# GateLoop attention and a squared-ReLU FFN on one core: scores as 64 by 64 tiles, the last store on SyncE, a new order for the first part

## The chip, the core and the metric

The kernel runs on one core of a Trainium2 chip. A core has a matrix engine (TensorE, "PE" in the profile, with its weight loads as "PEld"), VectorE (DVE), ScalarE (ACT), GpSimd (POOL) and SyncE (SP), which only issues transfers and waits. Each works through its own list of instructions in order and waits for others by semaphores. The metric is the device time of one execution in microseconds, the median of the runs.

## The reference

The first part is a linear attention with a complex gate for each step and channel; its result, rearranged, is the input of a two-layer FFN.

```
q, k, v, a_re, a_im: (B, H, S, D) = (4, 8, 768, 48), fp32
scale = min(|a|, 0.999) / (|a| + 1e-6);  a = (a_re + i a_im) * scale
for t in range(S):
    S_state = a[t] * S_state + k[t] outer v[t]      # complex state, (D, D) per head
    y[t]    = q[t] @ real(S_state)
x = y as (B*S, H*D) = (3072, 384)
h = relu(x @ w_in)            # w_in: 384 x 2048
out = (h * h) @ w_out         # w_out: 2048 x 384
```

The two weights come in double precision and are turned into fp32 on the core ("decoding"): each element is two 32-bit words.

## The kernel before

A sequence is cut into 6 chunks of 128 steps. Two sequences go together as a "group": there are 12 groups (`gi`), each with two chunks (`b` = 0 and 1), so 24 chunks. The first group of each pair of sequences begins with an empty state. The channels lie on the partitions as two heads of 48 rows, each in a half of 64 rows (`rows(hh)`); with four pairs of heads (`p_` = 0 to 3) all eight heads are there. The last pair lies in the gaps of the other three and is copied out of them into `last` by a transfer (`last_heads`, L901).

For each chunk the function `chunk` makes:

- `scores` (a0, b0): unless the chunk is the first of its sequence, the states' products `y` (L936), 16 matmuls of 48 rows by 64 columns; then the scores `a_ps` (L944), 16 matmuls of 48 rows by 128 columns, two parts of a complex product for four pairs and two heads.
- `keys_turned` and `keys_copied` (a1 to a4): transposes of the keys into `tp` (L951) and ScalarE's copies into `kt`.
- `masked` (a5): VectorE multiplies the scores by the causal mask.
- `sums_of_values` (a6), `tokens` (a7, ScalarE's copies into `x`), `added` and `new_state` (a8, a9).

Each fp32 matmul instruction leaves two records in the trace, so the 16 scores of a chunk are 32 records.

`make_operands` makes queries and keys with the gates' running products: 31 steps (tokens `o` for a whole group, `p` and `q` for the first and second half of the first two groups). Its last products, p30 and q30, release the transposes, the scores and the heads' copy (p21, q21).

The FFN follows group by group: `g` fills the gaps of `x` by a transfer (L1039), `F` is the first product `h_ps` (L1047 for the first two groups, L1063 later), `H` the squared ReLU (L1070, L1071), `T` or `Z` the second product (L1083, L1153), `R` its evacuation (L1026, L1029), `s` the store (L1117). X, Y and Q are sums on VectorE that save a part of the second product. In the first part of the run the weights are decoded block by block: `f` and `j` load the words (L692, L688), U and S are ScalarE's two steps (L618, L625), D and A VectorE's two (L632 and an addition at L494). `w` and `W` read the weights again to check their range; `K` reduces the check to one number, `count`.

The order of everything is one string, `FRONT`, that is followed token by token; each token adds its instructions to the lists of the engines that it uses, and the lists are kept in that order. `l` and `i` load the group's operands into `raw`, `v` loads the values into `vt`, and M0 to M8 are preparations: M0 is one small activation that brings in ScalarE's table for the reciprocal root, M1 makes the mask by two ScalarE copies with a transpose between, M2 to M8 are VectorE's memsets.

At the end each engine loads `count`, compares and branches past a general path (L1362, L1363) that these inputs do not take. Behind the branch SyncE goes through the semaphores of all queues and engines. The last group's second output tile is stored in two halves, of which ScalarE's queue issues the one that is ready last.

Of the kernel before, what the change touches and what calls it, by code (L numbers as in the profile page):

```python
# [32 lines left out]
ROWS = 64  # L33
LEVELS = 7
HALF = 64
RE, IM = 0, 1
# [390 lines left out]
def quotient_path(ctx, tc, feat, vtok, w_in, w_out, w1, w2, out, n_seq, count):  # L427

    nc = tc.nc
    N, _, D, _, NP, C = feat.shape  # L430
    DM, FF = w_in.shape
# [31 lines left out]
    def rows(hh):  # L463
        return head_rows(hh, D)
# [450 lines left out]
    def chunk(gi, b):  # L915
# [7 lines left out]
        def scores():  # L923
            qk = qk_of[gi % 2]

            def operand(i, p_, at):
                return last[gi % 2][at, b, i, 0:C] if p_ == NG else qk[at, b, p_, i, 0:C]

            ys = tiles["y"] = [py.tile([P, NP, C], F32, tag="y", name="y") for _ in range(2)]
            ps = tiles["ps"] = pa.tile([C, HH, NP, C], F32, tag="a", name="a_ps")  # L930
            if not first:
                for two in range(0, NP, 2):
                    for c in (RE, IM):
                        for hh in range(HH):
                            for p_ in (two, two + 1):
                                nc.tensor.matmul(  # L936
                                    ys[p_ % 2][crossed(hh, p_), p_ // 2],
                                    lhsT=states[b][1 - c_seq % 2][rows(hh), c, columns(hh, p_ * ROWS + PAD)],
                                    rhs=operand(c, p_, rows(hh)),
                                    start=(p_ < 2 and c == RE), stop=False, skip_group_check=True)  # L940
            for p_ in range(NP):
                for c in (RE, IM):
                    for hh in range(HH):
                        nc.tensor.matmul(ps[:, hh, p_], lhsT=operand(2 + c, p_, rows(hh)),  # L944
                                         rhs=operand(c, p_, rows(hh)), start=(c == RE),
                                         stop=(c == IM))

        def keys_turned(c):
            tp = tiles["tp"] = pm.tile([C, NG, P], F32, tag="m", name="tp")
# [161 lines left out]
    def store(i, b):  # L1111

        queue, cols = nc.sync, slice(0, DM)
        if i == NGR - 1 and b:
            queue, cols = (nc.scalar, slice(0, MH)) if b == 1 else (nc.sync, slice(MH, DM))
        b = min(b, 1)
        queue.dma_start(out=in_turn(out, groups[i][b])[:, :, cols], in_=out_of[i, b][:, cols])  # L1117

# [38 lines left out]
    def outputs(i, r):  # L1157
# [27 lines left out]


    FRONT = (
        "M8 l0.0.0 M2 M3 M7 l0.0.1 M1 M0 p0.0 p0.1 p0.3 p0.4 p0.5 p0.7 p0.2 q0.0 q0.3 p0.8 p0.9 "
        "p0.10 q0.4 q0.5 p0.11 q0.7 l0.1.0 f0 f1 l0.1.1 v0.0 f2 i0.1.0 j0 j2 q0.1 p0.12 p0.22 "
        "q0.8 q0.2 U0 q0.9 p0.6 q0.10 S0 p0.15 p0.23 p0.24 D0 p0.25 M4 p0.13 M5 p0.16 q0.11 "  # L1190
        "p0.26 i0.1.1 j1 D1 p0.27 A0 p0.17 p0.14 j3 i1.2.0 U1 S1 U2 q0.12 p0.18 q0.6 S2 q0.22 "
        "A1 f4 l1.2.0 f3 j4 p0.19 q0.15 p0.20 q0.23 p0.28 q0.24 p0.29 q0.25 p0.30 q0.16 D2 "
        "q0.26 q0.13 q0.27 A2 q0.17 p0.21 f6 a0.1 a0.2 U3 q0.14 a0.0 a0.3 U4 S3 q0.18 p1.6 a0.4 "
        "S4 a0.5 a0.6 l1.2.1 a0.7 D3 q0.19 M6 a0.8 q0.28 q0.20 p1.0 p1.3 q0.29 D4 q0.30 i1.2.1 "
        "q1.0 p1.4 p1.5 j6 j5 p1.1 p1.2 j7 g0.0 f5 v0.1 q0.21 f7 p1.7 p1.10 p1.9 p1.8 A3 A4 "
        "F0.1.0 U5 a0.9 U6 S5 D5 b0.1 b0.0 p1.11 b0.2 p1.12 S6 H0.1.0 A5 U7 b0.3 b0.4 S7 p1.15 "
        "D6 p1.23 b0.5 F0.0.0 b0.6 b0.7 f8 p1.24 A6 p1.25 q1.3 p1.16 D7 p1.26 A7 p1.27 D8 p1.17 "
        "F0.2.0 H0.0.0 q1.4 H0.2.0 U8 p1.22 S8 F0.3.0 b0.8 H0.3.0 p1.18 p1.13 p1.14 A8 g0.1 f11 "
        "F0.2.1 f9 f10 v1 p1.19 p1.20 p1.28 D9 p1.29 p1.30 q1.5 U9 q1.1 H0.2.1 q1.7 D11 b0.9 "
        "D10 F0.3.1 T0.0.0 H0.3.1 S9 A9 U10 q1.8 S10 q1.9 q1.2 q1.10 F0.0.1 F0.1.1 p1.21 f12 "  # L1200
        "f13 A10 q1.6 U11 q1.11 q1.12 S11 U12 a1.0 a1.1 T0.1.0 a1.5 a1.6 a1.7 S12 D13 D12 A11 "
        "q1.15 q1.23 A12 T0.2.0 T0.3.0 a1.2 U13 H0.0.1 q1.22 H0.1.1 a1.3 T0.4.0 q1.24 q1.25 "
        "q1.16 q1.26 q1.13 q1.27 q1.17 f14 g1.0 f15 S13 q1.14 l2 F1.2.0 H1.2.0 A13 F1.0.0 "
        "F1.3.0 q1.18 a1.4 U14 H1.3.0 U15 S14 i2 S15 q1.19 q1.28 q1.20 q1.29 D14 q1.30 A14 D15 "
        "A15 q1.21 a1.8 T0.5.0 F1.1.0 T0.6.0 T0.7.0 o2.0 o2.1 o2.3 o2.4 E0.0 o2.5 o2.2 b1.0 "
        "o2.7 a1.9 b1.5 T0.0.1 T0.1.1 b1.3 T0.2.1 b1.6 T0.3.1 T0.4.1 T0.5.1 T0.6.1 T0.7.1 o2.8 "
        "o2.9 o2.10 H1.1.0 b1.7 s0.0 v2 g1.1 w0 o2.11 o2.12 o2.15 o2.22 o2.13 o2.6 H1.0.0 "
        "F1.0.1 F1.1.1 E0.1 o2.14 b1.4 H1.1.1 l3 T1.0.0 b1.1 H1.0.1 F1.3.1 T1.1.0 T1.2.0 T1.3.0 "
        "T1.4.0 T1.5.0 T1.6.0 T1.7.0 o2.23 o2.24 o2.25 o2.16 o2.26 o2.27 o2.17 o2.18 o2.19 "
        "o2.28 o2.20 o2.29 o2.30 F1.2.1 o3.0 o3.6 o3.3 o3.4 o3.5 b1.2 o3.7 E1.0 b1.8 b1.9 o2.21 "  # L1210
        "a2.0 a2.5 t0 a2.1 T1.0.1 T1.1.1 o3.2 o3.1 o3.8 a2.2 o3.10 o3.9 a2.3 a2.6 a2.4 a2.7 "
        "H1.2.1 o3.11 o3.12 W0 a2.8 b2.0 a2.9 o3.22 H1.3.1 b2.5 T1.2.1 T1.3.1 b2.6 T1.4.1 "
        "T1.5.1 T1.6.1 b2.7 T1.7.1 g2 F2.0 o3.13 o3.15 o3.23 o3.24 o3.25 o3.16 o3.26 o3.27 "
        "o3.17 o3.14 H2.0 o3.18 o3.19 o3.28 o3.20 o3.29 o3.30 F2.2 H2.2 F2.4 H2.4 l4 s1.0 b2.1 "
        "F2.1 o4.0 H2.1 o3.21 s0.1 v3 F2.6 H2.6 b2.2 o4.3 F2.5 F2.7 o4.2 o4.4 o4.5 H2.7 X2.0 t1 "
        "X2.2 Y2.2 t3 H2.5 Y2.0 o4.7 b2.3 a3.0 b2.4 E1.1 s1.1 X2.1 Y2.1 a3.5 Z2.1 b2.8 a3.6 "
        "o4.1 o4.8 o4.9 Q2.0 b2.9 a3.3 a3.7 o4.10 a3.4 o4.11 F2.3 H2.3 Z2.0 a3.1 b3.0 X2.3 R2.0 "
        "o4.6 o4.22 Z2.3 a3.2 b3.5 b3.6 b3.7 o4.12 Y2.3 o4.13 Q2.3 Q2.1 o4.15 o4.23 Q2.2 o4.24 "
        "a3.8 a3.9 Z2.2 R2.3 Z2.5 o4.14 R2.2 R2.5 R2.1 o4.25 o4.16 o4.26 o4.27 o4.17 g3 F3.2 "
        "H3.2 F3.0 b3.3 b3.4 Z2.4 H3.0 o4.18 o4.19 o4.20 o4.28 o4.29 o4.30 F3.4 H3.4 F3.6 R2.4 "  # L1220
        "H3.6 X3.2 X3.0 F3.5 F3.1 b3.1 H3.5 F3.7 w1 l5 o5.0 t2 Z2.6 o5.3 o5.1 o5.4 H3.1 b3.2 "
        "o5.5 R2.6 o5.7 X3.1 o4.21 s2.1 s2.0 W1 w2 v4 F3.3 H3.3 H3.7 o5.2 Z3.0 b3.8 a4.0 X3.3 "
        "b3.9 Y3.1 Y3.2 a4.1 a4.5 Y3.0 Z3.1 R3.0 o5.6 o5.9 a4.2 o5.8 a4.3 Q3.0 o5.10 R3.1 o5.11 "
        "Q3.2 Y3.3 a4.6 a4.4 a4.7 a4.8 b4.0 a4.9 b4.1 Z3.2 Z3.3 o5.12 o5.22 b4.2 W2 b4.3 b4.4 "
        "R3.2 b4.5 b4.6 R3.3 b4.7 b4.8 o5.15 o5.23 o5.24 o5.25 Q3.1 Q3.3 o5.16 o5.13 Z3.4 Z3.5 "
        "w3 g4 o5.14 R3.4 o5.26 R3.5 F4.5 H4.5 l6 o5.27 o5.17 o5.18 o5.19 o5.20 v5 o5.28 F4.1 "
        "H4.1 X4.1 o5.29 F4.0 F4.4 o5.30 H4.0 o6.0 W3 H4.4 o6.3 b4.9 F4.3 Z3.6 H4.3 o6.4 F4.2 "
        "H4.2 o6.5 R3.6 o6.2 o6.1 F4.6 o6.7 H4.6 o5.21 s3.0 a5.0 F4.7 s3.1 o6.9 o6.8 a5.5 a5.6 "
        "o6.10 a5.7 H4.7 Z4.0 b5.0 Z4.1 Y4.1 o6.11 X4.3 Y4.3 X4.0 o6.6 w7 o6.22 o6.12 W7 R4.0 "
        "b5.5 X4.2 o6.15 Y4.0 Q4.0 R4.1 b5.6 Y4.2 Q4.1 Z4.2 R4.2 b5.7 o6.23 o6.24 Q4.2 o6.25 "  # L1230
        "o6.16 Z4.3 o6.13 Q4.3 o6.26 Z4.4 R4.3 Z4.5 R4.5 o6.27 o6.17 R4.4 o6.14 g5 F5.2 H5.2 "
        "o6.18 F5.4 F5.0 H5.4 o6.19 o6.28 o6.20 o6.29 o6.30 F5.3 Z4.6 l7 w6 H5.0 W6 a6.3 F5.1 "
        "o7.1 R4.6 H5.3 H5.1 F5.6 o7.0 H5.6 a6.4 X5.0 o7.3 o7.4 o7.5 F5.7 s4.0 o6.21 w8 v6 F5.5 "
        "a6.0 v7 a6.1 Z5.0 H5.5 W8 H5.7 o7.2 a6.2 w4 s4.1 X5.2 a6.5 Y5.0 Y5.2 o7.7 a6.6 a6.8 W4 "
        "o7.9 o7.8 R5.0 o7.10 b6.0 w9 W9 a6.7 Z5.1 X5.1 a6.9 b6.5 Q5.0 X5.3 Q5.2 Y5.1 Y5.3 R5.1 "
        "o7.11 Z5.2 o7.12 b6.3 R5.2 b6.4 Z5.3 b6.1 Z5.4 Q5.3 o7.15 o7.23 o7.24 o7.25 Q5.1 o7.16 "
        "w5 R5.3 b6.2 o7.22 W5 R5.4 b6.6 b6.8 Z5.5 Z5.6 b6.7 w10 g6 F6.1 o7.13 o7.26 o7.27 R5.5 "
        "o7.14 o7.6 o7.17 o7.18 o7.19 o7.28 o7.20 o7.29 o7.30 H6.1 F6.6 F6.5 l8 R5.6 H6.6 W10 "
        "v8 o7.21 s5.0 w14 s5.1 H6.5 F6.2 H6.2 F6.0 o8.0 o8.2 H6.0 b6.9 X6.2 Y6.2 o8.3 F6.4 "
        "a7.1 F6.3 o8.4 o8.5 H6.3 o8.6 H6.4 a7.0 a7.5 X6.1 a7.2 F6.7 H6.7 o8.1 X6.0 o8.7 o8.8 "  # L1240
        "o8.10 Z6.0 a7.3 R6.0 o8.9 Z6.1 Y6.0 X6.3 Y6.3 Y6.1 Q6.0 Q6.2 Z6.2 a7.4 W14 a7.6 a7.7 "
        "R6.2 a7.8 o8.11 a7.9 b7.0 Q6.3 R6.1 b7.5 w13 W13 o8.12 b7.1 b7.2 o8.22 Z6.3 R6.3 o8.13 "
        "o8.15 Q6.1 o8.23 o8.24 b7.6 b7.3 Z6.4 b7.7 b7.4 g7 o8.14 Z6.5 o8.25 R6.5 o8.16 o8.26 "
        "o8.27 o8.17 R6.4 b7.8 F7.5 F7.0 H7.5 o8.18 H7.0 F7.1 w15 W15 H7.1 l9 F7.4 o8.19 o8.28 "
        "o8.20 o9.0 H7.4 F7.2 F7.6 H7.2 o8.29 X7.1 o8.30 o9.3 o9.4 o9.5 o9.7 Y7.1 o9.1 Z6.6 "
# [150 lines left out]
```

## Time and profile before

| | |
|---|---|
| Median of 3 runs | 664.95 us (664.7 to 665.57) |
| The profiled execution | 666.06 us |
| Its span, first to last instruction | 664.1 us |
| Granted TensorE clock, mean | 0.996 |
| Busy, PE / DVE / ACT / POOL | 616.7 / 493.2 / 434.9 / 31.9 us |
| First transpose of keys | 35.55 us |
| Last matmul begins its group | 655.34 us |

The page divides the span into 40 slices of 16.6 us and gives the busy tenths of each engine. A row of the timeline has the start, the length, the engine, the line, the operation with its output and inputs, how many instructions it merges, and in brackets how long the engine had been idle before it and what ended that. Matmuls overlap, so the length of a merged row is not the sum of its parts; the distance of starts is what counts. Transfers have their own rows at the time of their issue (SPq, ACTq, POOL).

### The profile page before, as it was taken

The numbers are of one execution on the slowest core, as the hardware profiler recorded it, in microseconds if no ns is written. First come the engines' busy times: TensorE is split into PE (matmuls) and PEld (weight loads), VectorE is DVE, ScalarE is ACT, GpSimd is POOL, SyncE is SP. The second block draws the span as 40 slices with busy tenths as digits, with TensorE's granted clock in tenths as the row PEclk, the third lists the DMA queues.
The fourth block names the chain that finished last, engine by engine and source line by source line (L and its number), as shares of the span: only waits on it lengthen the run. The fifth ranks groups of instructions, "written<-read, shape, count | busy, mean of one in ns | idle before, by whom it ended". The sixth has DMA issues, their size and how long they took to land.

```text
span 664.1 us, 13108 instructions
## 1 busy us (share of the span) xinstructions
PE 616.7 (93%) x5147; PEld 552.0 (83%) x5147; DVE 493.2 (74%) x981; ACT 434.9 (65%) x847; POOL 31.9 (5%) x74
## 2 busy tenths in 40 slices
PE   0068999999999999999999999999999999999996
PEld 0057987776889899989899899899999899989996
DVE  4999888979997969858849948968849858753030
ACT  7668989757584585494586785686685675644331
POOL 5230110000000000000000000000000000000000
PEclk9998999999999999999999999999999999999999
DMA  8986863540634331730842813542631620232101
GB/s 198 167 160 148 257 192 68 92 56 21 95 72 82 55 87 32 119 73 10 142 142 55 142 51 79 96 109 72 113 95 32 108 65 21 67 84 79 47 26 30
DMA packets 41744, 60.41 MB, mean 91 GB/s; under 512 B 5832, under 2 KB 29896, under 8 KB 41672
## 3 DMA queue, kind: packets, MB, share of 16 engines
q1 hardware_dynamic: 39360, 55.39, 38.7%
q0 software_dynamic: 1824, 3.64, 3.0%
q8 instruction: 42, 0.69, 0.5%
q10 hardware_dynamic: 488, 0.44, 0.2%
q14 instruction: 30, 0.25, 0.1%
HBM read 48.76 MB, written 4.72 MB: 81 GB/s over the span
## 4 chain that ended last, share of the span: by engine, by line
PE 91%; DVE 5%; DMA 2%; ACT 1%; issue 1%; ACTq 0%; POOL 0%; DVEq 0%; SPq 0%
PE h_ps L1063 31%; PE o_ps L1153 28%; PE a_ps L944 7%; PE o_ps L1083 6%; PE h_ps L1047 6%; PE y L970 4%; PE y L936 3%; PE add L994 3%; PE tp L951 2%; DVE ab L494 1%; DMA last<-qk 1%; DVE pr L494 1%; DMA raw<-in_feat_dram 1%; DVE qk L494 0%; DMA words<-in_moe_w_in_dram 0%
## 5 line engine op out<-in xcount | busy, mean ns | idle before, releaser
L1063 PE MATMUL h_ps<-x,w 128*128 128x256 f32 x960 | 212.4, 379 | 0.0
L1063 PEld LDWEIGHTS h_ps<-x,w 128*128 128x128 f32 x960 | 180.9, 190 | 24.1 <-ACT h L1070 0.2
L1153 PE MATMUL o_ps<-w,h 128*128 128x192 f32 x640 | 110.5, 328 | 0.0
L1153 PEld LDWEIGHTS o_ps<-w,h 128*128 128x128 f32 x640 | 103.8, 190 | 1.9 <-issue 0.5
L1070 ACT ACTIVATE h<-h_ps 128x512 f32<-128x512 f32 x80 | 47.5, 594 | 69.5 <-PE h_ps L1063 67.3
L494 DVE TENSOR_TENSOR pr<-ab 128x384 f32<-128x384 f32 (+3 forms) x196 | 70.1, 375 | 4.3 <-ACT ab L833 0.9
L1153 PE MATMUL o_ps<-w_sum,mix 128*128 128x192 f32 x320 | 55.3, 328 | 0.0
L494 DVE TENSOR_TENSOR a<-a_ps,mask 128x1024 f32<-128x1024 f32 x24 | 29.3, 1222 | 33.6 <-PE a_ps L944 33.5
L494 DVE TENSOR_TENSOR ab<-pr 128x48 f32<-128x48 f32 (+3 forms) x210 | 49.9, 260 | 5.3
L1153 PEld LDWEIGHTS o_ps<-w_sum,mix 128*128 128x128 f32 x320 | 51.7, 190 | 0.7 <-issue 0.2
L1071 ACT ACTIVATE h<-h 128x512 f32<-128x512 f32 x80 | 50.5, 631 | 2.5
L951 PE MATMUL tp<-ident,qk 128*128 128x128 f32 x120 | 21.5, 291 | 30.3 <-DVE qk L494 30.0
L1047 PEld LDWEIGHTS h_ps<-x,w 128*128 128x128 f32 x384 | 45.6, 197 | 4.0 <-DVE w L494 1.3
L1047 PE MATMUL h_ps<-x,w 128*128 128x128 f32 x384 | 46.4, 281 | 2.2 <-DMA x<-x 1.1
L494 DVE TENSOR_TENSOR qk<-ab,qk 128x768 f32<-128x768 f32 (+1 forms) x56 | 46.1, 842 | 1.0
L1083 PE MATMUL o_ps<-w,h 128*128 128x384 f32 x128 | 44.3, 492 | 0.0
L951 PEld LDWEIGHTS tp<-ident,qk 128*128 128x128 f32 x120 | 14.8, 146 | 35.3 <-issue 31.7
L981 ACT COPY x<-y 64x256 f32<-64x256 f32 (+1 forms) x72 | 26.5, 368 | 24.9 <-PE y L970 23.4
L944 PE MATMUL a_ps<-qk 48*128 48x128 f32 x576 | 39.9, 287 | 0.0
L494 DVE TENSOR_TENSOR mix<-h 128x256 f32<-128x256 f32 x40 | 16.8, 420 | 30.9 <-ACT h L1071 30.9
L758 ACT ACTIVATE qk<-raw 128x768 f32<-128x768 f32 (+1 forms) x28 | 37.4, 1341 | 3.6 <-DVE raw L494 3.6
L494 DVE TENSOR_TENSOR room<-ab,carry 128x1344 f32<-128x1344 f32 (+1 forms) x28 | 36.8, 1354 | 3.6 <-ACT carry L874 2.8
(106 smaller groups left out, 923.4 us busy)
## 6 DMA issues: line engine op xcount, KB each, us to landing
raw<-in_feat_dram SPq DMA_DIRECT2D x40, 288.0 KB
words<-in_moe_w_out_dram SPq DMA_DIRECT2D x8, 768.0 KB
again<-in_moe_w_in_dram SPq DMA_DIRECT2D x16, 384.0 KB
again<-in_moe_w_out_dram SPq DMA_DIRECT2D x16, 384.0 KB
last<-qk SPq DMA_DIRECT2D x48, 97.5 KB
words<-in_moe_w_in_dram SPq DMA_DIRECT2D x8, 576.0 KB
vt<-in_vtok_dram SPq DMA_DIRECT2D x24, 192.0 KB
out_dram<-o SPq DMA_DIRECT2D x23, 192.0 KB
```

Of the source, the lines that this page charges most:

```text
L494: nc.vector.tensor_tensor(out=out, in0=in0, in1=in1, op=op)
L758: nc.scalar.activation(out=out.rearrange("p c j n -> p c n j"), func=AF.Copy, in_=in_.rearrange("p c (n j) -> p c n j", j=L), **kwargs)
L944: nc.tensor.matmul(ps[:, hh, p_], lhsT=operand(2 + c, p_, rows(hh)), rhs=operand(c, p_, rows(hh)), start=(c == RE), stop=(c == IM))
L951: nc.tensor.transpose(tp[:, g], qk_of[gi % 2][:, b, g, 2 + c, 0:C], ident)
L970: nc.tensor.matmul(tiles["y"][p_ % 2][crossed(hh, p_), p_ // 2], lhsT=v[:, columns(hh, at)], rhs=tiles["am"][:, hh, p_], start=(first and ...
L981: nc.scalar.copy(out=x_of[gi][to, odd::2, b * C:(b + 1) * C], in_=tiles["y"][odd][of, 0:NP // 2])
L1047: nc.tensor.matmul(ps[:, j], lhsT=w1_blocks[:, k, g, at:at + P], rhs=x_of[i][:, g, b * C:(b + 1) * C], start=(g == 0), stop=(g == NG - 1))
L1063: nc.tensor.matmul(ps[:, j], lhsT=w1_blocks[:, k, g, at:at + P], rhs=x_of[i][:, g], start=(g == 0), stop=(g == NG - 1))
L1070: nc.scalar.activation(out=h, in_=h_ps[i, f], func=AF.Relu, scale=of_w1)
L1071: nc.scalar.activation(out=h, in_=h, func=AF.Square)
L1083: nc.tensor.matmul(o_of[i, b], lhsT=tokens_of(i, f, b)[:, j], rhs=w2[:, k], start=(k == 0), stop=(k == NFB - 1))
L1153: nc.tensor.matmul(to, lhsT=x(k)[:, j], rhs=factor(z)[:, 2 * k + j], start=(z in (0, 1, 3) and k == j == 0), stop=(k == KH // 2 - 1 and j ...
```

## The change

It has three parts in the code. The scores' product is split into two halves of 64 columns each, so that each of the 16 matmuls becomes two, one for each half of the output partitions. The half store that ScalarE issued is issued by SyncE. And the first part of `FRONT`, up to the end of group 3's work, stands in another order; from `g4` on it is the same. Its description also names a warming of ScalarE's table ahead of the mask's copies.

```diff
             for p_ in range(NP):
                 for c in (RE, IM):
                     for hh in range(HH):
-                        nc.tensor.matmul(ps[:, hh, p_], lhsT=operand(2 + c, p_, rows(hh)),
-                                         rhs=operand(c, p_, rows(hh)), start=(c == RE),
-                                         stop=(c == IM))
+                        for s in (slice(0, ROWS), slice(ROWS, C)):
+                            nc.tensor.matmul(ps[s, hh, p_],
+                                             lhsT=operand(2 + c, p_, rows(hh))[:, s],
+                                             rhs=operand(c, p_, rows(hh)), start=(c == RE),
+                                             stop=(c == IM), skip_group_check=True)
...
         queue, cols = nc.sync, slice(0, DM)
         if i == NGR - 1 and b:
-            queue, cols = (nc.scalar, slice(0, MH)) if b == 1 else (nc.sync, slice(MH, DM))
+            cols = slice(0, MH) if b == 1 else slice(MH, DM)
         b = min(b, 1)
...
     FRONT = (
-        "M8 l0.0.0 M2 M3 M7 l0.0.1 M1 M0 p0.0 p0.1 p0.3 p0.4 p0.5 p0.7 p0.2 q0.0 q0.3 p0.8 p0.9 "
-        "p0.10 q0.4 q0.5 p0.11 q0.7 l0.1.0 f0 f1 l0.1.1 v0.0 f2 i0.1.0 j0 j2 q0.1 p0.12 p0.22 "
-        "q0.8 q0.2 U0 q0.9 p0.6 q0.10 S0 p0.15 p0.23 p0.24 D0 p0.25 M4 p0.13 M5 p0.16 q0.11 "
-        "p0.26 i0.1.1 j1 D1 p0.27 A0 p0.17 p0.14 j3 i1.2.0 U1 S1 U2 q0.12 p0.18 q0.6 S2 q0.22 "
-        "A1 f4 l1.2.0 f3 j4 p0.19 q0.15 p0.20 q0.23 p0.28 q0.24 p0.29 q0.25 p0.30 q0.16 D2 "
-        "q0.26 q0.13 q0.27 A2 q0.17 p0.21 f6 a0.1 a0.2 U3 q0.14 a0.0 a0.3 U4 S3 q0.18 p1.6 a0.4 "
-        "S4 a0.5 a0.6 l1.2.1 a0.7 D3 q0.19 M6 a0.8 q0.28 q0.20 p1.0 p1.3 q0.29 D4 q0.30 i1.2.1 "
-        "q1.0 p1.4 p1.5 j6 j5 p1.1 p1.2 j7 g0.0 f5 v0.1 q0.21 f7 p1.7 p1.10 p1.9 p1.8 A3 A4 "
-        "F0.1.0 U5 a0.9 U6 S5 D5 b0.1 b0.0 p1.11 b0.2 p1.12 S6 H0.1.0 A5 U7 b0.3 b0.4 S7 p1.15 "
-        "D6 p1.23 b0.5 F0.0.0 b0.6 b0.7 f8 p1.24 A6 p1.25 q1.3 p1.16 D7 p1.26 A7 p1.27 D8 p1.17 "
+        "l0.0.0 l0.0.1 M1 M0 p0.0 p0.1 p0.3 p0.4 p0.5 p0.7 M2 M3 p0.2 q0.0 q0.3 M8 M6 M7 p0.9 "
+        "p0.8 q0.4 p0.10 q0.5 p0.11 l0.1.0 f0 f1 f2 i0.1.0 j0 j2 q0.1 p0.12 q0.7 p0.15 D0 p0.23 "
+        "p0.24 p0.25 U0 q0.10 p0.6 p0.22 q0.8 p0.13 S0 q0.9 q0.2 p0.14 p0.16 A0 U2 p0.26 M5 j1 "
+        "i0.1.1 U1 S1 S2 D2 p0.27 q0.11 p0.17 j3 i1.2.0 j4 q0.12 p0.18 D1 q0.15 p0.19 l0.1.1 "
+        "q0.22 f3 l1.2.0 v0.0 f5 q0.23 p0.28 q0.24 M4 p0.20 q0.25 p0.29 q0.16 p0.30 q0.26 q0.13 "
+        "q0.27 p0.21 f4 a0.1 a0.0 A1 q0.17 a0.5 A2 q0.14 q0.6 p1.6 a0.2 U3 a0.3 a0.4 q0.18 S3 "
+        "a0.6 l1.2.1 q0.19 U4 a0.7 S4 D3 D4 A3 i1.2.1 j5 j6 j7 a0.8 p1.0 q0.28 p1.3 q0.20 q1.0 "
+        "D5 q0.29 q1.3 q0.30 U5 p1.4 p1.5 g0.0 f6 F0.1.0 S5 q0.21 p1.7 A4 a0.9 b0.1 p1.2 p1.10 "
+        "p1.8 p1.9 p1.1 U6 b0.2 p1.11 A5 b0.0 f7 v0.1 p1.12 H0.1.0 S6 U7 p1.22 p1.15 b0.5 p1.23 "
+        "D6 p1.24 D7 f8 F0.0.0 b0.6 b0.3 b0.7 S7 b0.4 H0.0.0 p1.25 A6 p1.16 A7 F0.2.0 b0.8 U8 "
...
```

## The prediction

> **What bounds the kernel now.** I read the page's rows of busy time and slices first, then sums over four stretches of the span, then the TensorE timeline, and last the end of the span.
>
> ```profile
> PE 616.7 (93%) x5147; PEld 552.0 (83%) x5147; DVE 493.2 (74%) x981; ACT 434.9 (65%) x847; POOL 31.9 (5%) x74
> PE   0068999999999999999999999999999999999996
> ...
> 35.50:62.00 26.50, 20.12 (x171) 17.92 (x172) 25.85 (x62) 22.46 (x42) 6.78 (x14) 0.94 0.82 174
> 62.00:656.00 594.00, 594.00 (x4966) 532.06 (x4965) 441.15 (x830) 388.15 (x758) 11.22 (x28) 1.00 0.38 82
> ```
>
> The stretch rows give PE, PEld, DVE, ACT, POOL, clock and DMA. From 62 to 656 us TensorE is busy for 594.00 of 594.00 us: there, what is taken off its stream is taken off the time, and nothing else counts. From 35.5 to 62 it is busy 20.12 of 26.50 us while VectorE has 25.85: there VectorE's order decides. Before 35.5 TensorE waits for the first operands.
>
> ```profile
> 185.51 0.76 PE L936 MATMUL y<-qk,state 48*64 48x128 f32 x17
> ...
> 186.54 1.61 PE L944 MATMUL a_ps<-qk 48*128 48x128 f32 x24
> 187.98 0.61 PE L944 MATMUL a_ps<-last 48*128 48x128 f32 x8
> 188.53 0.76 PE L1153 MATMUL o_ps<-w,h 128*128 128x192 f32 x3
> ```
>
> One chunk: 32 records of the states' products, in 64 by 64 tiles, take 1.03 us (185.51 to 186.54); 32 records of the scores, 128 columns wide, take 1.99 (to 188.53). The single starts say why. State products start four together, 109 ns from four to four; scores start two together, 111.7 ns from two to two. Where the form of tile changes there is a hole: the last four state products to the first two scores is 219 ns, those to the next two 213, the last two to o_ps 202.
>
> ```profile
> 48.77 1.58 PE L1047 MATMUL h_ps<-x,w 128*128 128x128 f32 x12 [1.12 <-DMA x<-x]
> 51.42 1.60 PE L1047 MATMUL h_ps<-x,w 128*128 128x128 f32 x12 [1.08 <-DVE w L494]
> ...
> 56.79 0.71 PE L944 MATMUL a_ps<-last 48*128 48x128 f32 x6 [0.27 <-DMA last<-qk]
> 57.43 0.83 PE L951 MATMUL tp<-ident,qk 128*128 128x128 f32 x3
> 58.05 4.24 PE L1047 MATMUL h_ps<-x,w 128*128 128x128 f32 x24
> ```
>
> The front: the first hidden product waits for the gap fill, then for a decoded weight block; the second chunk's scores wait for the heads' copy; and the 24 records at 58.05 take 177 ns each, against 132 at 48.77, because the clock is down (granted 0.72 over 56 to 62). Matmuls run at half speed from 35.5 to 47.4 and again from 57.6 to 61.0.
>
> ```profile
> 653.21 3.36 SPq L1117 DMA_DIRECT2D out_dram<-o  x2
> ...
> 658.14 0.33 ACT L1026 ACTIVATE o<-o_ps 128x192 f32<-128x192 f32 x1 [7.79 <-PE o_ps L1153]
> 658.50 1.20 ACTq L1117 DMA_DIRECT2D out_dram<-o  x1
> ...
> SPq L1363 <- SPq L1363: 4.6, 2, 3.9
> SPq L1392 <- ACTq L1363: 0.8, 1, 0.8
> ```
>
> The end (the last two rows are waits: total, times, longest). SyncE has issued its last store at 656.57, takes its branch, and stands 3.9 us[...] (660.5); then it goes through some twenty semaphores, and lastly waits 0.8 us for ScalarE, whose 1.20 us store issue put its own branch at 660.5.
>
> **The change part by part.**
>
> *Scores as 64 by 64 tiles.* 32 records become 64 per chunk. Today, counted from the last four state products to the matmul after the scores: 0.219 + 0.213 + 14 x 0.1117 + 0.202 = 2.20 us. After it: the form of tile no longer changes between state products and scores, so 16 fours at 0.109, then the hole to o_ps: 0.109 + 15 x 0.109 + 0.202 = 1.95. That is 0.25 less, in 20 chunks (the four that begin a sequence have no state products): 5.1 us. Two of those four (339 and 346 us) gain 0.1 each: the first step is 140 ns as with the state products, not 207, and 14 x 2.7 ns come on top. The other two are in the front. Sum -5.3. The streaming itself hardly gains; the two changes of form do. The mask's multiply comes 0.25 us earlier and is off the bound. The lower bound on the gain is 14 x 2.7 ns x 22 = 0.8 us, if the hole at the entry stays; I take the upper end, since the states' products are the same form on the same queue.
>
> [...] The row: 32 state products leave in 1.03 us, 32 ns apiece. [...] I use the row; but no row shows 96 such records one after another, as now come. That is the rival below.
>
> *The table load.* In both lists of ScalarE the order is load, the mask's two copies, load, the warming activation (3.27 to 7.42 us), and M1 stands ahead of M0 in both plans. This edit is not there: 0. Were it, at most the one 1.28 us load would leave the way to the first square at 7.33.
>
> *The front's order.* Up to the fourth product of the first half (the one that releases the first transpose, ended 35.4): VectorE gets one more pair of step instructions (0.64), one more first decode step (0.47) and one fewer second step (-0.87): +0.24. Memsets of 1.7 us move from idle time before 8.19 into that stretch. begun and qk (0.79) fill the 0.24 us hole before 11.38 and push by 0.5; states and kt (0.9) fill 0.8 us before 12.76. Start of TensorE: +0.75, so 36.3. In cold clock the scores end about 40.4, still ahead of the mask's multiply, which VectorE reaches at 42.3 as today; its work up to there is 0.8 us more, and the memsets fill as much of the 2.1 us of holes that it has today. Behind it the gain begins: the decode step that stalls the hidden product now ends at 47.8, not 51.4. ScalarE has more ahead of the tokens' copy (a decode step and the moved half's queries), so the gap fill lands about 1.1 later: product from 49.9 to 52.5, without the hole (today to 53.0). The second half's heads' copy can be issued only at 51.3 (today 49.4), but on SyncE's queue it no longer stands behind the 192 KB of vt, 1 us of transfer at the 174 GB/s of the stretch; I have it land near 55.5, not 56.8. Scores end about 56, the next product 58.5, the mask is there at 59.1 (59.8 today). With F0.2, F0.3 and add behind it, add ends near 67.4, today 69.9: -2.5. Bounds: -5 (the 6.4 us of idle less the 1.1 us that come first, or a second cold spell avoided too), +2 (VectorE's later start not recovered). No row shows the new order, and I keep the middle, as the DVE rows behind 42 us carry it. Queues passed: SyncE's third words load goes ahead of one raw half, used at 38 us only; GpSimd issues one words pair ahead of another. From 67 us on TensorE covers the rest as before; if a list beyond that leaves it waiting, that adds in full.
>
> *The last store on SyncE.* ScalarE saves its 1.20 us issue and is no longer the last to come. SyncE issues at 658.5 (0.64 us, as its own store rows), and takes its branch behind it, 2.6 us later than now. The row is the stall of 3.9 us behind it[...]. With 3.9: 659.2 + 3.9 + 1.35 (the semaphores without their waits) = 664.4, where SyncE is through at 663.25 today: +1.2. With ScalarE's own stall, 2.6: -0.1. Three engines branch together today and two will, so I take +0.5 and keep both ends.
>
> **Sum.** -5.3 - 2.5 + 0.5 = -7.3 us. The profiled execution took 666.06 us (span 664.1 and 1.96 around it), 1.1 above the median 664.95 of three; it would become 658.8. On the median: 657.7 us.
>
> **The rivals.**
> 1. *Front worth nothing*: the later start is not made up, or a wait comes back later in the list. Scores and end alone: -4.8, 660.2 us. For it: VectorE is the bound to 62 us and has more to do. Against: the 51.42 hole is cut by 3.6 us of VectorE's order.
> 2. *More from the front*: the second cold spell (3.4 us at half speed, 1.7 us lost) is avoided, and the copy lands earlier: -10, 655 us.
> 3. *Slower: TensorE's instruction feed.* States' products and scores now ask for 96 records in 2.9 us[...]. [...] For it: the densest long run today is 112 records in 5.13 us, 46 ns each. Against: the last states' products of that run still come at 27 ns.
> 4. *Not what it says*: the tiles don't run four together or the hole stays; gain 0.8 only, front and end as above: 662.2 us.
>
> **How the numbers follow.** The forecast has 0.55, rival 2 0.12, rival 1 0.18, rival 4 0.06, rival 3 0.04; 0.05 for a front that loses 2 to 5 us, of which some reaches no change (664 to 665). About 0.2% (1.3 us) is what a measurement of this kernel can tell from no change. Faster 0.91, same 0.03, slower 0.06. The range runs from the middle of rival 2 with the front's lower bound, 654.6, past rivals 1 and 4 to 662.4.
>
> **What the profile of the changed kernel would show.** Right: a_ps x64 in about 1.75 us behind y, starts in fours, no 0.2 us hole between them; first transposes near 36.3; no wait on a decode step in the first hidden product; busy PE without idle from about 58; SyncE's branch wait after a store at 658 less the gain, and no wait for ScalarE at the end. Wrong: scores above 2.0 us, holes in TensorE between 67 and 300 us, a first transpose after 38.

## The result and the profile after

| | before | changed | ratio |
|---|---|---|---|
| Median | 664.95 us (664.63 to 665.57, 5 runs) | 660.88 us (659.33 to 662.53, 5 runs) | 0.994 (0.9924 to 0.9956) |
| The profiled execution | 666.06 | 659.33 | |
| Its span | 664.1 | 657.0 | |

The change gains 4.1 us, where 7.3 were forecast. The profiled execution fell by 6.7, nearly the forecast; it is the fastest of the changed kernel's five, as that of before was slower than all five of its own. So the difference of the two traces is not the difference of the medians, and most of what follows is about that.

The changed kernel's page, its row of busy times and its queue of TensorE's instructions (packets, MB, share):

```profile
PE 610.1 (93%) x5915; PEld 548.3 (83%) x5915; DVE 492.0 (75%) x981; ACT 434.7 (66%) x847; POOL 35.9 (5%) x74
...
q8 instruction: 48, 0.79, 0.5%
```

Its sums over two stretches (PE, PEld, DVE, ACT, POOL, clock, DMA share, GB/s):

```profile
35.50:62.00 26.50, 20.96 (x260) 18.83 (x261) 25.81 (x60) 23.48 (x47) 9.05 (x14) 0.94 0.79 176
62.00:649.00 587.00, 586.84 (x5647) 527.73 (x5646) 440.60 (x830) 387.24 (x755) 13.28 (x28) 1.00 0.39 83
```

From 62 us on TensorE is still the bound: 586.84 of 587.00 us busy. In the front, VectorE still has 25.8 of 26.5 us. There are 768 more matmul records (5915 for 5147) and as many more weight loads, and six more packets of instructions (48 for the 42 of before), which will matter. That the queue is TensorE's is inferred from that number: it rises by six with the split scores, so by one for each 256 of the 1536 new records, and its first packet behind 35 us comes at 51.4 us before and at 46.4 with the split scores alone, but at 52.3 and 51.1 with the new order or the store alone.

The clock column counts only from the first change to full speed on. Ahead of it the sums print 1.00, and half speed is read off the records: at 36.17 us three transposes take 0.87 us, at 54.54 us 0.52.

One chunk, the same as in the prediction, on TensorE's timeline of the changed kernel:

```profile
184.20 0.76 PE L936 MATMUL y<-qk,state 48*64 48x128 f32 x17
...
185.13 1.49 PE L945 MATMUL a_ps<-qk 48*64 48x128 f32 x48
186.44 0.61 PE L945 MATMUL a_ps<-last 48*64 48x128 f32 x16
186.98 0.48 PE L1065 MATMUL h_ps<-x,w 128*128 128x256 f32 x1
```

States' products take 0.93 us to the first score (1.03 before), the 64 score records 1.85 (1.99 before). In the single records the scores start four together, 7 ns apart, 108 ns from four to four, and the first four follow the last four states' products like any others: the 219 ns hole where the form of tile changed is gone, and the exit is still about 200.

The front, on TensorE's timeline of the changed kernel:

```profile
36.17 0.87 PE L953 MATMUL tp<-ident,qk 128*128 128x128 f32 x3 [30.69 <-DVE qk L494]
...
49.28 4.37 PE L1049 MATMUL h_ps<-x,w 128*128 128x128 f32 x24 [2.45 <-DVE room L787]
54.54 0.52 PE L953 MATMUL tp<-ident,qk 128*128 128x128 f32 x3 [0.90 <-DVE pr L494]
54.99 1.54 PE L945 MATMUL a_ps<-qk 48*64 48x128 f32 x48
56.35 0.61 PE L945 MATMUL a_ps<-last 48*64 48x128 f32 x16
56.89 2.94 PE L1049 MATMUL h_ps<-x,w 128*128 128x128 f32 x24
```

Neither the decoded block nor the heads' copy stops TensorE any more. Two things are new: the first hidden product is at half speed from 50.5 us on (182 ns a record on average), and the second chunk's transposes wait 0.90 us for VectorE, which has yet to read the PSUM tile of the first chunk's `add` that `tp` shares.

The end, SyncE's own waits in the last 17 us:

```profile
SPq L1365 <- SPq L1365: 2.9, 1, 2.9
SPq L1119 <- ACT o L1028: 1.8, 1, 1.8
SPq L1394 <- PEq L1394: 0.7, 2, 0.5
```

The wait for ScalarE at the end is gone, as said (the second row is the wait for the last evacuation), and the stall behind SyncE's branch is 2.9 us in this execution (3.9 before).

### The profile page after: what moved, and what is told of

The parts are those of the page before. It is cut to its first block, busy times and chain, and to the rows that moved or that the text cites. A ratio compares the mean times of both kernels' runs of the same rounds, so it can differ in the third digit from the quotient of the medians.

```text
span 657.0 us, 14644 instructions
## 1 busy us (share of the span) xinstructions
PE 610.1 (93%) x5915; PEld 548.3 (83%) x5915; DVE 492.0 (75%) x981; ACT 434.7 (66%) x847; POOL 35.9 (5%) x74
## 4 chain that ended last, share of the span: by engine, by line
PE 89%; DVE 6%; ACT 1%; DMA 1%; issue 1%; ACTq 0%; DVEq 0%
PE h_ps L1065 32%; PE o_ps L1155 28%; PE o_ps L1085 6%; PE h_ps L1049 6%; PE a_ps L945 6%; PE y L972 4%; PE y L936 3%; PE add L996 3%; PE tp L953 2%; DVE ab L494 1%; DVE pr L494 1%; DMA raw<-in_feat_dram 1%; DVE w L494 1%; DVE qk L494 1%; DVE room L494 0%
## 5 line engine op out<-in xcount | busy, mean ns | idle before, releaser
L494 DVE TENSOR_TENSOR ab<-pr 128x48 f32<-128x48 f32 (+3 forms) x210 | 49.9, 260 | 5.3
L1073 ACT ACTIVATE h<-h 128x512 f32<-128x512 f32 x80 | 50.5, 631 | 2.5
L953 PEld LDWEIGHTS tp<-ident,qk 128*128 128x128 f32 x120 | 14.9, 145 | 37.0 <-issue 33.7
L758 ACT ACTIVATE room<-z 128x768 f32<-128x768 f32 (+1 forms) x28 | 36.7, 1371 | 5.1 <-DVE z L805 5.1
L945 PE MATMUL a_ps<-qk 48*64 48x128 f32 x1152 | 38.1, 275 | 0.0
```

What stands on the lines that cost most here:

```text
L494: nc.vector.tensor_tensor(out=out, in0=in0, in1=in1, op=op)
L758: nc.scalar.activation(out=out.rearrange("p c j n -> p c n j"), func=AF.Copy, in_=in_.rearrange("p c (n j) -> p c n j", j=L), **kwargs)
L945: nc.tensor.matmul(ps[s, hh, p_], lhsT=operand(2 + c, p_, rows(hh))[:, s], rhs=operand(c, p_, rows(hh)), start=(c == RE), stop=(c == IM), ...
L953: nc.tensor.transpose(tp[:, g], qk_of[gi % 2][:, b, g, 2 + c, 0:C], ident)
L1073: nc.scalar.activation(out=h, in_=h, func=AF.Square)
```

## The experiments

### Each part alone

```diff
 e1_scores_only: before, with the scores' loop of the change
 e1_front_only:  before, with FRONT of the change
 e1_store_only:  before, with
-            queue, cols = (nc.scalar, slice(0, MH)) if b == 1 else (nc.sync, slice(MH, DM))
+            cols = slice(0, MH) if b == 1 else slice(MH, DM)
 e1_after_again: the changed kernel
```

> The kernel before with the scores as 64 by 64 tiles and nothing else. The trace of the changed kernel has states' products and scores of a chunk in 2.79 us where they took 3.02. Theory A (the tiles alone account for it, in every execution): 18 chunks by 0.23, 2 by 0.08 and about 0.1 for the two cold ones, -4.5 us, 660.4 us against 664.95. Rival B (TensorE's gain is given back, since something else than TensorE is late once it runs ahead): between -1 and -3 us, and holes in TensorE between 67 and 600 us that the kernel before does not have.

> The kernel before with the new order of the first part and nothing else. Theory A (the front is worth what the profiled execution showed): -2.5 to -3 us, 662.2 us. Rival C (the profiled execution of the changed kernel is the fastest of five, 1.5 us under their median, and the front is what varies): 664 to 666 us in the median and a spread of 2 us or more, where the kernel before spreads 1 us.

> The kernel before with the last half store on SyncE and nothing else. The prediction has +0.5 us (-0.1 to +1.2): 665.4 us. In the changed kernel's trace SyncE's branch waits 2.9 us, where it waited 3.9, and the way from the last evacuation to the end is 6.1 us against 6.0. Theory A: +0.1 us, 665.1. Rival D (the stall behind SyncE's branch is 3.9 us in most executions): +1 us, 666.0.

> The changed kernel once more, for a second trace and five more times. Theory A: 657.7 us as predicted, the first five having fallen high by chance. Rival C (the front varies): median 660 to 661.5 with 2 us or more between the fastest and the slowest, and a trace in which a wait in the front, or the cold clock, stands elsewhere than in the first trace.

| | median | ratio to before (665.31, 27 runs) | in us |
|---|---|---|---|
| scores alone | 660.78 | 0.9936 (0.9924 to 0.9948) | -5.1 to -3.5 |
| front alone | 665.60 | 1.0007 (0.9998 to 1.0016) | -0.1 to +1.1 |
| store alone | 665.67 | 1.0002 (0.9994 to 1.0011) | -0.4 to +0.7 |
| changed kernel again | 660.71 | 0.9933 (0.9920 to 0.9946) | -5.3 to -3.6 |

The scores alone are the whole change: the three parts add up to -3.9 us, and the changed kernel has -4.1 and -4.6. In the trace of the scores alone a chunk's states' products and scores take 2.78 us (3.02 before), and the scores of the two chunks at full speed that have no states' products take 1.91 (1.99); 20 x 0.24 and 2 x 0.08 make 4.9. The new order is worth nothing in the median, and the store nothing that can be measured. Rival C's median came true for the front and for the changed kernel.

Why the front is worth less than forecast is seen in the trace of the store alone, which has the front of before. Its TensorE timeline:

```profile
48.82 5.18 PE L1047 MATMUL h_ps<-x,w 128*128 128x128 f32 x24 [1.05 <-DMA x<-x]
...
57.64 2.84 PE L1047 MATMUL h_ps<-x,w 128*128 128x128 f32 x24
```

In the profiled execution of before these were 12 records, a wait of 1.08 us for a decoded block, 12 records, and later 24 records in 4.24 us at half speed. Here the first product is at half speed and in one piece: it is so slow that the block is decoded in time, so the hole that the new order removes is not there. And the second spell of half speed is not there. Nor do the traces of the scores alone and of the old order in the last table below have that hole or that spell. The sums over the two stretches show it, first for the store alone, then for before (the sixth number is the granted clock):

```profile
57.60:61.00 3.40, 3.40 (x36) 3.28 (x36) 3.33 (x8) 3.29 (x6) 0.00 (x0) 1.00 0.52 204
```

```profile
57.60:61.00 3.40, 3.40 (x17) 3.40 (x17) 3.33 (x7) 2.94 (x6) 0.00 (x0) 0.50 0.60 220
```

Same code, 36 records for 17 in the same 3.4 us. The start of the 13th chunk's scores gives what each execution's front was worth: from there on the lists are the same, and TensorE is the bound.

| front | execution | 13th chunk's scores, us | full speed from |
|---|---|---|---|
| old | before | 339.15 | 47.3, half speed again 57.6 to 61.0 |
| old | store alone | 338.22 | 53.3 |
| new | front alone | 337.31 | 54.5 |
| old | scores alone | 335.75 | 53.3 |
| new | changed | 333.87 | 47.1, half speed again 50.5 to 53.9 |
| new | changed, again | 334.56 | 55.1 |

Against the profiled execution of before the new front is 1.84 us ahead. Against the old front without the second spell it is 0.9 ahead (338.22 to 337.31), and with split scores 1.2 to 1.9 (335.75 to 334.56 and 333.87). The time outside the span takes 0.37 us back: it was 1.92 to 2.01 us in each of the traces with the old order, 2.28 to 2.30 in each with the new one, and it differs in the same way in the runs that were not traced (1.9 to 2.1, and 2.2 to 2.4). What lies in it the trace does not show.

The spells end and begin at steps of 3.41 us within an execution (47.31, 57.55 and 60.97 us before, three steps and one; 47.07, 50.48 and 53.89 changed, one step each), and lie elsewhere in the next: in its second trace the changed kernel is at full speed from 55.1 on, without a second spell. Why they lie where they do the traces do not show. Between the executions of before and of the store alone, which differ in the spells and in the hole, the difference was 0.93 us at the 13th chunk.

### A busier TensorE, the table, and the order of the tiles

```diff
 e2_before_spin, e2_after_spin: in chunk(), for the first chunk only
+        def spin(times):
+            idle = tiles["idle"] = po.tile([P, DM], F32, tag="o", name="idle")
+            for _ in range(times):
+                nc.tensor.matmul(idle[:, 0:C], lhsT=ident, rhs=begun[:, E - C:E], start=True,
+                                 stop=True)
+        # 13 ahead of the first transposes, 8 behind the second, 12 behind the add
 e2_after_table: the changed kernel, with
-        "l0.0.0 l0.0.1 M1 M0 p0.0 ...
+        "l0.0.0 l0.0.1 M0 M1 p0.0 ...
 e2_scores_apart: the changed kernel, with
-                for c in (RE, IM):
+                for s in (slice(0, ROWS), slice(ROWS, C)):
                     for hh in range(HH):
-                        for s in (slice(0, ROWS), slice(ROWS, C)):
+                        for c in (RE, IM):
```

> The kernel before, and 33 idle matmuls of 128 by 128 by 128 on TensorE in its three idle stretches (ahead of the first transposes, behind the second, and behind the first add); their product is never read. Theory E (the granted clock makes the front's length: with TensorE busy it is at full speed before the first hidden product, and no second spell of half speed comes): the first hidden product is at 132 ns a record and shows the wait for the decoded block at 50 to 51.4 us; the heads' copy, landed at 56.8, then bounds the front, so 0.5 to 1 us less than before (664.5) and a spread under 1 us. Rival F (the clock is not what varies; VectorE's order and the copies set the front): 665.3 and the same spread, or slower by the idle matmuls that come late, up to +1 us.

> The changed kernel with the same 33 idle matmuls. Theory E: the first hidden product takes 2.7 us in one piece, without the wait for a decoded block, and TensorE then waits for VectorE's state at 54.5; 659.3 us or a little less (the fastest of the changed kernel's runs), spread under 1.5 us. Rival F: 660.8 and a spread of 3 us as the changed kernel, or up to +1 us.

> The changed kernel with the table's warming activation ahead of the mask's two copies, which its description names and its code does not do. ScalarE's list then has one table load less, 1.28 us. If the first square (7.31 us) follows and the features are there by 6.0, VectorE and the first transposes come 1.3 us earlier (34.9 us for 36.2), and the end by 0.5 to 1 us: 660 us. If the features land only at 7, or VectorE is bound by its own work from 20 us on, nothing: 660.8.

> The changed kernel with the 64 records of scores of a pair of heads in another order: the halves of columns are outermost, then the heads (the halves of rows), and the two parts of the product innermost, so that four tiles which follow each other stand in two quarters of the array, not in four. Theory A (the 1.86 us of a chunk's scores come from four tiles in the four quarters that start together): two or fewer at a time, over 2.9 us instead of 1.86, +25 us or more, 685 us. Rival G (any 64-column matmuls would do): 1.86 us again, 660.8.

| | median | range | ratio to before (665.32, 14 runs) |
|---|---|---|---|
| before, busier | 667.00 | 664.97 to 668.94 | 1.003 (1.0017 to 1.0044) |
| changed, busier | 662.54 | 661.20 to 663.00 | 0.9953 (0.9940 to 0.9967) |
| changed, table first | 660.34 | 659.50 to 661.05 | 0.9932 (0.9918 to 0.9945) |
| scores apart | 663.52 | one run | |

*Busier.* Theory E's times did not come: both lose about 1.7 us, and the busier kernel before spreads over 4 us. Its condition was not met either: the clock was full early (from 33.7 us in the changed kernel), but did not stay so, and a front at full speed throughout was not seen. TensorE's timeline of the busier changed kernel:

```profile
49.28 2.84 PE L1062 MATMUL h_ps<-x,w 128*128 128x128 f32 x24
54.51 0.87 PE L963 MATMUL tp<-ident,qk 128*128 128x128 f32 x3 [2.39 <-DVE pr L494]
55.32 2.84 PE L945 MATMUL a_ps<-qk 48*64 48x128 f32 x48
57.93 1.08 PE L945 MATMUL a_ps<-last 48*64 48x128 f32 x16
58.94 3.92 PE L1062 MATMUL h_ps<-x,w 128*128 128x128 f32 x24
```

Its sum over the last spell of half speed:

```profile
54.20:61.00 6.80, 6.49 (x76) 5.86 (x77) 5.90 (x12) 6.57 (x13) 1.25 (x2) 0.50 0.88 238
```

The fast first product only makes TensorE wait longer (2.39 us) for VectorE, which has read the `add` at the same 54.4; behind that wait come 6.8 us of half speed. The saving on TensorE had nowhere to go. In the kernel before, the idle matmuls themselves came at half speed and pushed the first product to 51.56.

*Table first.* ScalarE's timeline has one table load, and the first square starts 1.48 us earlier (5.83 for 7.31):

```profile
3.25 1.28 ACT L558 ACT_TABLE_LOAD   x1 [3.25 <-issue]
4.54 0.20 ACT L558 ACTIVATE sums<-tiny 128x1 f32<-128x1 f32 x1
4.65 0.39 ACT L569 COPY mask<-plain 128x128 f32<-128x128 f32 x1
5.61 0.37 ACT L573 COPY mask<-turned 128x128 f32<-128x128 f32 x1 [0.57 <-PE turned L572]
5.83 0.84 ACT L773 ACTIVATE room<-raw 128x768 f32<-128x768 f32 x1
```

TensorE's timeline of the same kernel shows how far that carries:

```profile
34.89 0.88 PE L953 MATMUL tp<-ident,qk 128*128 128x128 f32 x3 [29.32 <-DVE qk L494]
...
43.64 1.89 PE L996 MATMUL add<-vt,kt 128*64 128x48 f32 x32
49.14 5.30 PE L1049 MATMUL h_ps<-x,w 128*128 128x128 f32 x24 [3.60 <-DMA x<-x]
```

The first transposes and the `add` come 1.3 us earlier; the first hidden product does not (49.14 for 49.28), and the median falls by 0.4 to 0.5 us, within the intervals. Something else than VectorE sets 49 us: the gap fill, issued at 44.43, landed at 48.89 and used at 49.14.

*Scores apart.* 2.01 us for a chunk's scores instead of 1.86, so 2.7 us slower than the changed kernel (one run), not 25. Theory A's number fell, and rival G is not right either. TensorE's timeline:

```profile
186.04 1.53 PE L945 MATMUL a_ps<-qk 48*64 48x128 f32 x46
...
187.46 0.66 PE L945 MATMUL a_ps<-last 48*64 48x128 f32 x14
188.06 2.86 PE L1065 MATMUL h_ps<-x,w 128*128 128x256 f32 x12
```

The single records start 6 to 69 ns apart, not in fours, yet still about four in 109 ns. By that rate tiles of different quarters seem to overlap although neighbours in the program share a quarter (a record does not name its quarter). The order costs 0.16 us, not a factor: two steps of four take 137 ns, and the last four start over 118 ns instead of 20.

### The fill and TensorE's instruction block

In the traces one thing goes with a late fill. TensorE's queue of instructions fetches in packets of 16 KB (48 for 0.79 MB), and those in the table took 1.3 to 1.5 us each. The first fetch behind 35 us comes after 197 to 238 rows of weight loads and matmuls in the traces below, so more records early bring it forward. The fill's second transfer leaves sixteen marks of landing in each trace, which the timeline does not print and which are taken here as one for each of sixteen parts; the last column has how far the last mark of the fill's second transfer lies behind the other fifteen.

| execution | fetch at, us | fill issued | second issue took | first hidden product | from issue | last mark |
|---|---|---|---|---|---|---|
| before | 51.4 | 46.00 | 0.58 | 48.77 | 2.8 | 0.06 |
| store alone | 51.1 | 45.95 | 0.58 | 48.82 | 2.9 | 0.01 |
| front alone | 52.3 | 45.70 | 0.58 | 48.63 | 2.9 | 0.09 |
| scores alone | 46.4 | 45.98 | 1.66 | 49.87 | 3.9 | 0.14 |
| changed | 46.0 | 45.73 | 1.29 | 49.28 | 3.6 | 0.01 |
| changed, again | 46.8 | 45.68 | 0.58 | 50.17 | 4.5 | 0.94 |
| changed, table first | 46.1 | 44.43 | 0.66 | 49.14 | 4.7 | 0.89 |

In each of these the product starts 0.09 us (old order) or 0.25 us (new order) behind the fill's last mark, so the fill is what it waits for, whatever a row's bracket names. The fetch shows in two ways. Where it begins 0.25 to 0.45 us ahead of SyncE's second issue (scores alone, changed), that issue takes 1.3 to 1.7 us instead of 0.6. Where it begins 0.4 to 0.9 us behind that issue's start (changed again, table first), one of the sixteen parts lands 0.8 to 0.9 us behind the others, in both transfers. One of the page's 16 DMA engines, taken by the fetch, could look like that; it is my reading and was not shown, since the trace does not number the engines. Why an issue is slow it does not show either.

Of the last four kernels two moved the fetch away, and the others separate the new order and the store on a base with the table first.

```diff
 e3_best_new: the changed kernel, M0 ahead of M1, the last store on nc.scalar as before
 e3_best_pad: that, and in M1 behind the mask's second copy
+        idle = po.tile([P, DM], F32, tag="o", name="idle")
+        for _ in range(24):
+            nc.tensor.matmul(idle[:, 0:C], lhsT=ident, rhs=ident, start=True, stop=True)
 e3_best_pad_state: that, and in FRONT
-  A4 a0.9
+  a0.9 A4
 e3_best_old: e1_scores_only, M0 ahead of M1
```

> The changed kernel with the warming activation ahead of the mask's copies and the last half store back on ScalarE. Against the changed kernel with the warming alone (660.34 us): the last matmul to the end took 6.4 to 6.7 us in the traces with ScalarE's store and 6.5 to 7.2 with SyncE's. Theory A (the store costs 0.4 us on SyncE): 659.9 us. Rival D (no difference): 660.3.

> The same with 24 idle matmuls on TensorE at 5 us, where it stands idle until 35; their product is never read. They move TensorE's instruction blocks of 16 KB by 6 KB, and so the fetch that runs at 46 us in every kernel with the split scores (and at 51 to 52 in those without) ahead of the first gap fill, to about 39. Theory H (that fetch, 1.3 to 1.5 us on one of the 16 DMA engines, delays the gap fill, which lands 2.8 us after its issue where there is no fetch and 3.5 to 4.7 where there is one): the first hidden product at 47.5 us instead of 49.1, and 0.5 to 1 us less at the end, 659.2. Rival I (the fill is late by the transfers of the operands ahead of it): 49 us and 659.9.

> The scores as 64 by 64 tiles, the warming activation first, the last store on ScalarE, and the old order of the first part: the pair to the first kernel of this call for the new order alone. The traces so far put the new order 0.9 to 1.9 us ahead inside the span, and 0.37 us behind outside it. Theory J (the new order is worth about 1 us): 660.9 us. Rival C (nothing): as the first, 659.9. The prediction's 2.5: 662.4.

> The padded kernel with VectorE's new state of the first chunk ahead of one decode step (0.95 us) that stands before it. The second chunk's transposes wait for it at 54.5 in the changed kernel (53.2 with the warming first), since they use the PSUM tile that it reads. If VectorE's order bounds there once the fill is early: transposes 0.9 us earlier, 658.5 us. If the cold first product (5.2 us from 47.5) bounds: as the padded kernel. If the decoded block is then late: up to +1.

| | median | range | ratio to before (664.98, 11 runs) |
|---|---|---|---|
| table first, ScalarE's store | 660.22 | 658.79 to 661.64 | 0.9930 (0.9916 to 0.9944) |
| the same, padded | 659.77 | 658.94 to 661.93 | 0.9921 (0.9908 to 0.9935) |
| the same, old order, not padded | 659.63 | 658.87 to 660.63 | 0.9921 (0.9908 to 0.9934) |
| padded, state ahead | 659.46 | 659.24 to 660.67 | 0.9921 (0.9909 to 0.9934) |

The four are one number within their intervals. The old order is at least as good as the new one (659.63 and 660.22), so 2.5 us for it is excluded a second time. TensorE's timeline unpadded and padded:

```profile
48.97 5.46 PE L1049 MATMUL h_ps<-x,w 128*128 128x128 f32 x24 [3.60 <-ACT part L618]
```

```profile
48.09 4.55 PE L1052 MATMUL h_ps<-x,w 128*128 128x128 f32 x24 [2.27 <-DMA x<-x]
53.57 0.52 PE L956 MATMUL tp<-ident,qk 128*128 128x128 f32 x3 [0.93 <-DVE pr L494]
...
90.64 8.28 PE L1052 MATMUL h_ps<-x,w 128*128 128x128 f32 x72 [0.75 <-DMA x<-x]
```

In the first row the bracket names ScalarE, but the fill's last mark is at 48.72, 0.25 us ahead of the product; it lies 1.05 us behind the other fifteen, with the fetch at 45.8. With the fetch moved to 37.9 us in both padded kernels, the product follows the fill's issue by 3.3 us (44.75 to 48.09) and 2.9 (45.35 to 48.21), not by 4.7 (44.27 to 48.97) as without the pad. The late part shrinks to 0.41 and 0.02 us. So theory H is right in direction: of the 1.4 us between the first pair, 0.6 is the one late part; the other 0.7, by which all parts land sooner, is not told apart. The padded kernel issues its fill 0.5 us later, so its product comes only 0.9 us earlier.

For the end it is worth little, since the next waits are right behind: 0.93 us for VectorE's state, and 0.75 us for the third gap fill at 90.64, issued at 85.53 with a later fetch at 87.7 beside it. The unpadded kernel, 0.9 us later at 80 us, has no such wait; its fetches there are at 83.0 and 93.8. With the state ahead the transposes wait no more (52.66), and TensorE waits 0.65 us for the mask's multiply at 58.6 instead.

## Why the prediction was right and where it was not

The time fell in the range and the direction was right; the likeliest number was 3.2 us too low, and the median stands at rival 1, the front worth nothing (660.2 forecast, 660.9 measured).

- *Scores, -5.3.* Measured -4.5 (3.5 to 5.1) alone. The mechanism was right: form changes, not streaming. The size per chunk was 0.24 for 0.25 with states' products and 0.08 for 0.1 without (20 x 0.25 is 5.0, not 5.1). The 96 records in a row leave in 2.78 us, 29 ns each (64 in 3.02 us before), and no hole comes between the two groups. Rival 3 and rival 4 are out.
- *Front, -2.5.* This step failed. Its single times were mostly met: first transposes 36.17 (36.3 forecast), mask 41.9 (42.3), decoded block 48.1 (47.8), first product 49.28 and 50.17 in two traces (49.9), heads' copy issued at 51.53 (51.3). Wrong was what they were compared with. "The decode step that stalls the hidden product" and the half speed from 57.6 are from one execution of before, and the store alone, with the same front, has neither; counted from it the new order is 0.9 us ahead (338.22 to 337.31), not 2.5. I took 7.3 us from the median although I had written that the profiled execution was 1.1 us above it: 0.93 us of the excess (339.15 for 338.22) lay in the very stretch that the change rewrites. I also took the first product to end at 52.5, at full speed; mostly at half speed it ended at 53.6 and 55.4. The step that I did not see is the PSUM tile by which the second chunk's transposes hang on VectorE's state, which the new order puts 1.2 us later; it cost 0.90 us in the first trace and nothing in the second, where the product itself ended later.
- *Still open in the front.* The traces of the new order show 0.9 to 1.9 us gained inside the span, and 0.37 lost outside the span; the medians show from 0.1 gained to 1.1 lost with the front alone. The spans of all runs agree with the medians: the middle one is 663.3 us with the front alone and 663.4 before, while the traced execution has 662.6 and is the third fastest of thirteen. Each trace of the changed kernel, the front alone, and the first kernel of the last table lies 0.4 to 1.6 us under its own median. So what the slower executions of these kernels lose is not known. A lower granted clock goes with it in the front alone, whose two slowest runs (667.40 and 668.01) have 0.992 and 0.991 and the other eleven 0.996 to 0.999, but not in the changed kernel, whose two slowest of eleven (662.53 and 662.75) have 0.996 and 0.999. Two executions above their median are traced with the new order, both with idle matmuls added: the busier one (0.5 above) has its 6.8 us of half speed, the padded one (0.8 above) its wait of 0.75 us at 90.64, which the trace with the state ahead does not have.
- *Store, +0.5.* Alone +0.36 (-0.4 to +0.7). From the last matmul's start to the end of the span it was 6.3 to 7.0 us in eight traces with ScalarE's store (mean 6.58), 6.5 to 7.2 in six with SyncE's (mean 6.93): 0.35 us, near the value taken. The stall behind SyncE's branch goes with the store: 3.9 to 4.0 us in all eight, 2.9 to 3.5 in all six (mean 3.3). So it lies between the two ends that the forecast kept (3.9 and 2.6), where a loss of 0.5 puts it. Why it is shorter is not shown.
- *Table, 0.* Right: it is not in the code. Done, it brings the transposes 1.3 us forward and the end at most 0.5.

## What to carry to other kernels

Before a part of one trace is counted as a gain, ask whether it is there in a second execution: if the profiled run is above its median, look for the excess in the stretch that the change rewrites, for it cannot be saved twice. In this front, where TensorE, VectorE and small transfers take turns, a microsecond taken from one of them mostly became a wait for the next, while a fraction of a microsecond in a block that repeats on the bound engine came through: 22 chunks with up to 0.24 us each gave 4.5. When small matmuls follow others, try the same form of tile for both; here 0.2 of the 0.24 us were the two holes at the change of form.

## What the hardware showed that was not expected

- More instructions on TensorE move its 16 KB fetch: from 51.4 us before to 46.4 with the split scores alone, and to 37.9 with the idle matmuls of the padded kernels. Where it fell on a small transfer, the product that needs the transfer came 3.6 to 4.7 us after its issue instead of 2.8 to 3.3. Either one of the transfer's sixteen parts landed about 1 us behind the rest, or the issue itself took 1.3 to 1.7 us instead of 0.6.
- Tiles of 64 by 64 in the four quarters kept nearly their rate without being neighbours in the program: 2.01 us for 64 records in the worse order, 1.86 in the better.
- SyncE's stall behind its taken branch was 3.9 to 4.0 us in every trace with ScalarE's last store, and 2.9 to 3.5 in every trace with SyncE's.
- Idle matmuls did not keep the clock up. In the busier changed kernel full speed came at 33.7 us, was lost at 40.5, came back at 44.0, and was lost from 54.2 to 61.0 around a wait of 2.4 us.
